# Attention and two gated FFNs on one core: the first four heads' gates by an added product, and the normalisation's small steps as one operation

## The chip, the cores and the metric

The kernel runs on one core of one Trainium2 chip, in one launch. The metric is the device time of the launch in microseconds (us); a kernel's time is the median of several runs. PE is TensorE, ACT is ScalarE, DVE is VectorE, POOL is GpSimd, and SP is the engine whose queue issues all DMAs here.

## What is computed

```python
# 4 batches, 8 heads, 576 tokens, head size 64
scores = q @ k.T / 8
cum    = np.cumsum(np.maximum(s, 0), axis=-1)              # gates, one row per head
scores = np.where(causal, -1e9, scores + np.minimum(-(cum[:, :, :, None] - cum[:, :, None, :]), 0))
attn   = np.exp(scores - scores.max(-1, keepdims=True))
attn   = attn / (attn.sum(-1, keepdims=True) + 1e-9)
x      = (attn @ v), heads side by side                    # 2304 tokens x 512
xn     = x / np.sqrt(np.mean(x * x, -1) + 1e-6) * rms_g
x      = (silu(xn @ w_gate) * (xn @ w_val)) @ w_out        # first FFN, 512 -> 1536 -> 512
out    = (silu(x @ w2_gate) * (x @ w2_val)) @ w2_out       # second FFN, no norm
```

All data are fp32. Because of the causal mask a query's own gate is a constant of its row, so only the keys' gates, less a common value, need to be added to the scores before the softmax.

## The kernel before

**Precision.** A dense product is made of three products of halves, high times high, low times high and high times low (`xH·H`, `xL·H`, `xH·L` in the rows). The weights are fetched raw and turned into the halves `H` and `L` on the chip by ACT (L384, L386, L396), DVE (L389, L392, L400) and POOL.

**Tiling.** Each batch's queries are two groups: A, the first 256 (tiles 0 and 1 of 128), and B, the other 320 (tiles 2 to 4). Group A of batches 0 and 1 is done first, as 16 early heads (`EarlyUnit`) in plain fp32 products. Then come the other groups head by head (`Head`, `Unit`).

**An early head.** `load` (L697) issues three DMAs: q and k transposed into rows 0 to 63 of a buffer `lq` (L701, 128 KB), the head's row of cumulated gates into row 64 of the key half (L705, 1 KB), and v into `vl` (L708). Row 64 of the query half holds ones and the rows behind are cleared by POOL (`clear_rows`, L457 and L458), so that the product over 128 rows adds each key's gate to its scores. `scores` (L711) makes two products, 128 x 128 and 128 x 256 (L716), into PSUM tiles `sps`. `least` (L601, DVE) adds the mask and finds each row's extreme in the same pass, and `exponent` (L612, ACT) writes the exponentials and their sums `tot`. `values` (L722) makes three transposes (L726), copies them to `pTA` (L731), makes the two products with v (L736) and copies the result into `x`. Two `lq` buffers of two halves each hold the loads of four heads.

**The gates.** The sequence `s` of all 32 heads is one 32 x 576 tile `cum`: clamped at zero (L473), cumulated by a scan (L476), reduced by its middle column and scaled (L481), all on DVE. It is stored to `cum_d` (L484) for the later heads.

**The normalisation** (`normalise`, L750) is called eight times, once for each group of each batch. ACT squares `x` (four operations), PE sums the squares with the constant `half` (L767) into one of four PSUM banks named `mo`, and 20 small steps of DVE (L795 to L829; tiles `fac`, `rc`, then the halves `sq`) make each token's factor for each head: inverse of the softmax sum, mean square, an inverse square root by three Newton steps, and the product of both. PE transposes the factors (L833), ACT copies them, PE spreads them over the rows by four products with the constant `sel` (L840), DVE multiplies `x` (L844), ACT and POOL or DVE make the halves `xH` and `xL` (L847, L849). Then the first FFN of this group may begin.

**The first FFN** (`moe1`): for each of 12 slices `f`, 12 products of `gate_value` (L860) fill one `mo` bank and 12 more a second one. `hidden` makes tanh (L867, ACT) and two operations of DVE (L869 `t`, L872 `hh`), which free the banks. `hh` is stored to `h_d`. The banks of the normalisation are out of the same four.

**What sets the order.** Nothing is issued as the code stands. Each operation is entered in a `Plan` with its engine, an assumed cost in ns, what it reads and writes, and a priority. `Plan.run` walks through an assumed time: an engine that is free takes the ready operation with the lowest priority value, and this writes out the fixed order of every engine. An operation entered as one is never split. `port=True` means that it isn't begun on DVE while POOL, by the plan, runs an operation. Each step of the normalisation is entered by itself:

```python
def step(fn, r=(), w=None):
    w = [col] if w is None else w
    op(DVE, TINY, fn, r=[*w, *r], w=w, pri=pri, port=True)   # TINY = 70
```

Of the kernel before, what the change touches and what calls it, by code (L numbers as in the profile page):

```python
# [251 lines left out]


@with_exitstack
def tile_kernel(
# [164 lines left out]

    mask = buf("at", "ft", [P, 2 * P], F32, "mask")

    def setup():
# [29 lines left out]

        def clear_rows(en):
            for b in early_q:
                for c in (0, 288):
                    en.memset(b()[D:, :, c:c + 256], 0.0)  # L457
                    en.memset(b()[D:D + 1, 0, c:c + 256], 1.0)  # L458
# [9 lines left out]
        def clear_scores(en):  # L468
# [4 lines left out]
        op(DVE, 400, lambda en: en.tensor_scalar(  # L473
            out=cum(), in0=cum(), scalar1=0.0, scalar2=None, op0=ALU.max),
           r=[cum], w=[cum], pri=-1e6)
        op(DVE, 670, lambda en: en.tensor_tensor_scan(  # L476
            cum2(), cum(), cum(), 0.0, op0=ALU.add, op1=ALU.max),
           r=[cum], w=[cum2], pri=-1e6)


        op(DVE, 400, lambda en: en.tensor_scalar(  # L481
            out=cum(), in0=cum2(), scalar1=cum2()[:, S // 2:S // 2 + 1], scalar2=1.0 / SCALE,
            op0=ALU.subtract, op1=ALU.mult), r=[cum2], w=[cum], pri=-1e6)
        op(SP, 4 * NB * NH * S, lambda en: en.dma_start(out=cum_d, in_=cum()),  # L484
           r=[cum], w=["cum_d"], pri=-1e6)
# [185 lines left out]
    class EarlyUnit(Unit):  # L671
# [6 lines left out]
        def __init__(self, b, h, x, tot):  # L678
# [8 lines left out]
            self.parts = lq_parts(early_q[i % 2], i // 2 % 2)  # L687
            self.vl = early_v[i % 2], i // 2 % 2
# [10 lines left out]
        def load(self, pri):  # L699
# [11 lines left out]
        def scores(self, pri):  # L711
            for t in self.tiles:
# [5 lines left out]
                    start=True, stop=True), r=[*self.parts, "lower rows"], w=[pt], pri=pri)  # L718
# [30 lines left out]
    def normalise(i, g, tot, pri):  # L749
# [42 lines left out]
        def u():  # L792
            return fac()[:, 1, :nt]
        F, U = (fac, 0), (fac, 1)
        step(lambda en: en.tensor_scalar(out=over(), in0=tot()[:, :nt], scalar1=1.0e-9,  # L795
                                         scalar2=None, op0=ALU.add), [tot], [F])
        step(lambda en: en.reciprocal(over(), over()), [], [F])
        step(lambda en: en.tensor_tensor(out=u(), in0=squares(), in1=over(), op=ALU.mult),
             [ps, F], [U])
# [342 lines left out]
```

## Time and profile before

| | |
|---|---|
| median of 3 runs | 1151.41 us (1149.88 to 1152.21) |
| the profiled execution's own time | 1150.37 us |
| its span, first to last instruction | 1148.4 us |
| mean granted clock of PE | 0.996 |
| PE busy | 1119.2 us, 97% of the span |
| DVE, ACT, POOL busy | 607.3, 545.7 and 188.9 us |

The profile is that of one execution. Its own time is 1.04 us below the median of the runs, and its span is 1.97 us shorter than its own time. Busy times are sums over the span; the stretches differ much, so they are read stretch by stretch in the rows below. Ends of products are modelled, since PE overlaps one product with the next.

### The profile page before, as it was taken

How to read it: one execution, taken by the hardware profiler on the slowest of the kernel's cores; microseconds unless marked ns; L12 is line 12 of the kernel's file. 1: busy time of each engine (PE TensorE's matmuls, PEld its weight loads, DVE VectorE, ACT ScalarE, POOL GpSimd, SP SyncE). 2: the span in 40 equal slices, each digit the busy share in tenths (PEclk: the TensorE clock that was granted, in tenths of full speed). 3: DMA queues.
4: the chain of work that ended last, by engine and by line, in shares of the span. 5: the costliest groups of instructions: out<-in, count | busy, mean ns of one | idle time of the engine just before them, and what ended most of it. 6: DMA issues, size and time to landing. Idle time of an engine off the chain costs nothing.

```text
span 1148.4 us, 18814 instructions
## 1 busy us (share of the span) xinstructions
PE 1119.2 (97%) x6708; PEld 1001.1 (87%) x6708; DVE 607.3 (53%) x1672; ACT 545.7 (48%) x1203; POOL 188.9 (16%) x282
## 2 busy tenths in 40 slices
PE   5889999999999999999999999999999999999998
PEld 3589999899999999999888788888888888888898
DVE  5898899979735875542686424432222222222222
ACT  5886889889434854431697435432111211211121
POOL 3343455354211300000021000001000100100000
PEclk9899999999999999999999999999999999999999
DMA  4874455334321223338756634211000100100000
GB/s 147 249 239 123 143 142 156 116 104 116 87 72 49 74 89 112 116 119 267 231 163 197 208 122 123 74 37 49 25 1 1 65 1 1 46 1 1 1 37 20
DMA packets 70221, 112.54 MB, mean 98 GB/s; under 512 B 11696, under 2 KB 39344, under 8 KB 70128
## 3 DMA queue, kind: packets, MB, share of 16 engines
q1 hardware_dynamic: 70128, 111.35, 31.6%
q8 instruction: 53, 0.87, 0.3%
q14 instruction: 40, 0.33, 0.1%
HBM read 87.63 MB, written 23.67 MB: 97 GB/s over the span
## 4 chain that ended last, share of the span: by engine, by line
PE 89%; DMA 3%; DVE 3%; ACT 2%; issue 1%; SPq 1%; POOL 0%; DVEq 0%; ACTq 0%
PE mo L860 50%; PE sps L1019 8%; PE tp L1019 8%; PE mo L1019 6%; PE sps L575 4%; PE tp L639 4%; PE tp L655 4%; DMA cvs<-in_w_gv 1%; PE mo L767 1%; PE tp L736 1%; PE sps L716 1%; DVE sc L601 1%; DMA hh<-h_d 1%; DMA lq<-cum 1%; PE tp L726 0%
## 5 line engine op out<-in xcount | busy, mean ns | idle before, releaser
L860 PE MATMUL mo<-xH,H 128*128 128x320 f32 (+1 forms) x768 | 228.1, 298 | 0.1
L860 PE MATMUL mo<-xL,H 128*128 128x320 f32 (+1 forms) x768 | 227.1, 296 | 0.5 <-POOL xL L849 0.5
L860 PE MATMUL mo<-xH,L 128*128 128x320 f32 (+1 forms) x768 | 227.0, 296 | 0.0
L869 DVE SCALAR_TENSOR_TENSOR t<-t,mo 128x256 f32<-128x256 f32 (+2 forms) x156 | 81.3, 521 | 257.7 <-ACT t L867 257.3
L867 ACT ACTIVATE t<-mo 128x256 f32<-128x256 f32 (+2 forms) x156 | 72.2, 463 | 284.8 <-PE mo L860 284.4
L860 PE MATMUL mo<-x1H,L 128*128 128x512 f32 (+1 forms) x480 | 176.6, 368 | 0.0
L860 PE MATMUL mo<-x1H,H 128*128 128x512 f32 (+1 forms) x480 | 176.6, 368 | 0.0
L860 PE MATMUL mo<-x1L,H 128*128 128x512 f32 (+1 forms) x480 | 176.6, 368 | 0.0
L1008 ACT ACTIVATE hH<-hh 128x512 fp32r<-128x512 f32 (+1 forms) x120 | 69.8, 585 | 169.4 <-DVE hh L872 133.1
L860 PEld LDWEIGHTS mo<-xL,H 128*128 128x128 f32 x768 | 144.2, 188 | 1.5 <-POOL xL L849 0.7
L860 PEld LDWEIGHTS mo<-xH,H 128*128 128x128 f32 x768 | 144.1, 188 | 1.0 <-issue 0.3
L860 PEld LDWEIGHTS mo<-xH,L 128*128 128x128 f32 x768 | 144.2, 188 | 0.4
L872 DVE TENSOR_TENSOR hh<-t,mo 128x256 f32<-128x256 f32 (+2 forms) x156 | 81.3, 521 | 99.4 <-PE mo L860 98.1
L1010 DVE TENSOR_TENSOR hL<-hh,hH 128x512 fp32r<-128x512 f32 (+1 forms) x120 | 79.6, 664 | 90.7 <-ACT hH L1008 90.3
L860 PEld LDWEIGHTS mo<-x1L,H 128*128 128x128 f32 x480 | 90.5, 189 | 15.0
L860 PEld LDWEIGHTS mo<-x1H,L 128*128 128x128 f32 x480 | 90.5, 189 | 14.9
L860 PEld LDWEIGHTS mo<-x1H,H 128*128 128x128 f32 x480 | 90.5, 189 | 14.7
L612 ACT ACTIVATE sc<-sc,col 128x512 f32<-128x512 f32 (+4 forms) x160 | 95.6, 598 | 15.6 <-DVE col L601 15.1
L1051 POOL TENSOR_TENSOR x1L<-x1l,x1H 128x512 fp32r<-128x512 f32 (+1 forms) x20 | 25.0, 1260 | 391.5 <-ACT x1H L1049 222.0
L639 PE MATMUL tp<-ident,sc 128*128 128x128 f32 x432 | 69.0, 278 | 1.3 <-DVE x L664 1.1
L1019 PE MATMUL sps<-hL,oH 128*128 128x512 f32 (+1 forms) x192 | 69.6, 364 | 0.1
L1019 PE MATMUL tp<-hL,oH 128*128 128x512 f32 (+1 forms) x192 | 69.4, 363 | 0.0
(129 smaller groups left out, 2097.0 us busy)
## 6 DMA issues: line engine op xcount, KB each, us to landing
raw<-in_w_gv SPq DMA_DIRECT2D x40, 512.0 KB, 4.8
cvs<-in_w_o SPq DMA_DIRECT2D x24, 512.0 KB, 3.7
hh<-h_d SPq DMA_DIRECT2D x48, 256.0 KB, 2.9
cb<-cum_d SPq DMA_DIRECT2D x32, 288.0 KB, 3.4
lq<-in_qk SPq DMA_DIRECT2D x32, 288.0 KB, 3.0
h_d<-hh SPq DMA_DIRECT2D x72, 128.0 KB, 2.2
vl<-in_vp SPq DMA_DIRECT2D x32, 160.0 KB, 3.1
cvs<-in_w_gv SPq DMA_DIRECT2D x8, 512.0 KB, 4.0
```

The source lines that it names most:

```text
L575: op(PE, c_mm(n), lambda en, pt=pt, o=o, c=c, n=n, z=z, kk=kk: en.matmul(pt()[:, :n], qst[j]()[:, o:o + 128], kk()[:, c:c + n], start=z == ...
L612: op(ACT, c_act(o + m, 2) + 35, lambda en: en.activation(sc()[:m, :o + m], sc()[:m, :o + m], ACTF.Exp, scale=-1.0, bias=col()[:m, 0, t:t + 1],
L639: op(PE, C_TR, lambda en, pt=pt, a=a, m=m, kb=kb, t=t: en.transpose(pt()[:, a:a + P], self.sc[t]()[:, kb * P:kb * P + P], ident()), r=[sel ...
L655: op(PE, c_mm(n), lambda en, w=w, z=z, kb=kb, d0=d0, n=n, o=o, kn=kn: en.matmul(po()[:, o:o + n], vst[j]()[:kn, kb, :], pT[g][z]()[:kn, d0 ...
L860: op(PE, c_mm(n), lambda en, a=a, x=x, c=c, k=k, i=i: en.matmul(ps()[:, :n], a()[:, c], x()[:, k, :n], start=(k == 0 and i == 0), stop=(k ...
L867: op(ACT, c_act(n), lambda en: en.activation(t()[:, :n], gp()[:, :n], ACTF.Tanh, scale=0.5), r=[gp], w=[t], pri=pri)
L869: op(DVE, c_tt(n), lambda en: en.scalar_tensor_tensor(out=t()[:, :n], in0=t()[:, :n], scalar=1.0, in1=gp()[:, :n], op0=ALU.add, op1=ALU.mu ...
L872: op(DVE, c_tt(n), lambda en: en.tensor_tensor(out=hh()[:, :n], in0=t()[:, :n], in1=vp_()[:, :n], op=ALU.mult), r=[vp_, t], w=[hh], pri=pri)
L1008: op(ACT, c_act(n) + 35, lambda en: en.activation(H()[:, :n], hh()[:, :n], ACTF.Copy), r=[hh], w=[H], pri=pri)
L1010: op(DVE, c_tt(n), lambda en: en.tensor_tensor(out=L()[:, :n], in0=hh()[:, :n], in1=f32(H()[:, :n]), op=ALU.subtract), r=[hh, H], w=[L], p ...
L1019: op(PE, c_mm(n), lambda en, d=d, c=c, w=w, x=x, i=i: en.matmul(acc_[d]()[:, :n], Wo[w]()[:, c], HL[x]()[:, :n], start=(f == 0 and i == 0) ...
L1051: op(POOL, c_ptt(n), lambda en, k=k, x=x: en.tensor_tensor(out=L()[:, k, :n], in0=x()[:, :n], in1=f32(H()[:, k, :n]), op=ALU.subtract), r= ...
```

## The change

1. The first four heads (`FIRST = 4`) get no row of gates by DMA. The cumulated gates of all 32 heads, for the first 256 keys, lie in a tile `cumA` of 128 rows, whose rows 32 to 127 are cleared by two memsets of POOL ahead of all other clearing. Behind each score product of these heads a second product adds `cumA`'s row of the head to all queries, with a column of the identity, spread, as the other operand. The other early heads' DMA reads its row out of `cumA`.
2. The three steps on the gates are made by `cumulate`, first for 256 columns into `cumA`, then once more for all 576 into `cum`, whose store to `cum_d` has a later priority.
3. In `normalise` two steps (the inverse) are one operation of the plan, and the other 18 are one, `factors`, entered at 170 ns for each step and without `port`.
4. The first FFN's weights have other priorities, both for the load and for the work on them.

```diff
+        def clear_cum(en):
+            en.memset(cumA()[NB * NH:64], 0.0)
+            en.memset(cumA()[64:], 0.0)
+        op(POOL, 500, clear_cum, w=[(cumA, 1)], pri=-2e6)
...
+        def cumulate(out, n, pri):
+            rows = NB * NH
+
+            def steps(en):
+                en.tensor_scalar(out=cum()[:, :n], in0=cum()[:, :n], scalar1=0.0, scalar2=None,
+                                 op0=ALU.max)
+                en.tensor_tensor_scan(cum2()[:, :n], cum()[:, :n], cum()[:, :n], 0.0,
+                                      op0=ALU.add, op1=ALU.max)
+                en.tensor_scalar(out=out()[:rows, :n], in0=cum2()[:, :n],
+                                 scalar1=cum2()[:, n // 2:n // 2 + 1],
+                                 scalar2=1.0 / SCALE, op0=ALU.subtract, op1=ALU.mult)
+            op(DVE, 400 + 3.6 * n, steps, r=[cum], w=[cum, cum2, (out, 0)] if out is not cum
+               else [cum, cum2], pri=pri)
+        cumulate(cumA, 2 * P, -1e6)
+        cumulate(cum, S, -900)
         op(SP, 4 * NB * NH * S, lambda en: en.dma_start(out=cum_d, in_=cum()),
-           r=[cum], w=["cum_d"], pri=-1e6)
+           r=[cum], w=["cum_d"], pri=-990)
...
-            op(SP, 1024, lambda en: en.dma_start(
-                out=ql()[D:D + 1, 1, 288 * i:288 * i + 256], in_=cum()[n:n + 1, 0:256]),
-               r=[cum, "lower rows"], w=self.parts[2:], pri=pri)
+            if not self.first:
+                op(SP, 1024, lambda en: en.dma_start(
+                    out=ql()[D:D + 1, 1, 288 * i:288 * i + 256], in_=cumA()[n:n + 1]),
+                   r=[cumA, "lower rows"], w=self.parts[2:], pri=pri)
...
+                if self.first:
+                    i = self.b * NH + self.h
+                    op(PE, 0.422 * 4 * kl, lambda en, pt=pt, kl=kl: en.matmul(
+                        pt()[:, :kl], ident()[:, i:i + 1].to_broadcast([P, P]), cumA()[:, :kl],
+                        start=False, stop=True), r=[ident, cumA], w=[pt], pri=pri)
...
-        def step(fn, r=(), w=None):
-            w = [col] if w is None else w
-            op(DVE, TINY, fn, r=[*w, *r], w=w, pri=pri, port=True)
+        chain = []
+
+        def step(fn):
+            chain.append(fn)
...
+        def inverse(en):
+            en.tensor_scalar(out=over(), in0=tot()[:, :nt], scalar1=1.0e-9, scalar2=None,
+                             op0=ALU.add)
+            en.reciprocal(over(), over())
+        op(DVE, 4 * TINY, inverse, r=[tot], w=[F], pri=pri, port=True)
...
+        def factors(en):
+            for fn in chain:
+                fn(en)
+        op(DVE, 170 * len(chain), factors, r=[ps, F], w=[col, fac, rr], pri=pri)
...
-        W1.append(load_gv(w_gv, f, places, tmps1, P_ATT + 10 + 0.5 * f,
-                          P_ATT - 1000 + 6 + 1.5 * f))
+        W1.append(load_gv(w_gv, f, places, tmps1, P_ATT + 12 + 0.5 * f,
+                          P_ATT - 1000 + 8 + 1.0 * f))
```

The costs and priorities change the order that the plan writes. On PE, at the very start of the program, the order before begins as follows (a number behind a name is that of the buffer's use; `lq_101` and `lq_106` are the first two heads):

```order
L716 MATMUL sps_165<-lq_101 128x128
L716 MATMUL sps_168<-lq_101 128x256
L716 MATMUL sps_177<-lq_106 128x128
L726 MATMUL tp_181<-ident,sc_170 128x128
L716 MATMUL sps_185<-lq_106 128x256
L726 MATMUL tp_181<-ident,sc_179 128x128 x2
```

After the change the same place on PE reads as follows, where L739 is the added product:

```order
L733 MATMUL sps_149<-lq_116 128x128
L733 MATMUL sps_162<-lq_116 128x256
L739 MATMUL sps_149<-cumA,ident 128x128
L739 MATMUL sps_162<-cumA,ident 128x256
L733 MATMUL sps_176<-lq_121 128x128
L739 MATMUL sps_176<-cumA,ident 128x128
L733 MATMUL sps_182<-lq_121 128x256
L749 MATMUL tp_187<-ident,sc_169 128x128
L739 MATMUL sps_182<-cumA,ident 128x256
```

Each score tile of the first four heads takes two products instead of one, eight added in all. On DVE, at the last of the eight normalisations, the 18 steps before stand among other work (L389 and L392 belong to weights, L872 to the first FFN). Nine of them stand here; nine more follow among other work, to L829:

```order
L798 TENSOR_TENSOR fac_5991<-mo_5931,fac_5991 128x24
L800 TENSOR_TENSOR fac_5991<-fac_5991 128x24
L872 TENSOR_TENSOR hh_6199<-t_6170,mo_6166 128x256
L801 TENSOR_REDUCE rc_6205<-fac_5991 128x3
L803 TENSOR_SCALAR rc_6205<-rc_6205 128x3
L805 TENSOR_SCALAR rc_6205<-rc_6205 128x3
L807 TENSOR_SCALAR rc_6205<-rc_6205 128x3
L810 SCALAR_TENSOR_TENSOR rc_6205<-rc_6205 128x3
L812 TENSOR_TENSOR rc_6205<-rc_6205 128x3
L389 TENSOR_SCALAR cvs<-cvs 128x512
L813 SCALAR_TENSOR_TENSOR rc_6205<-rc_6205 128x3
L392 SCALAR_TENSOR_TENSOR cvy<-cvy,cvs 128x512
```

After the change the 18 steps stand without a gap, and the FFN's two rows stand behind them; here is the end of the block:

```order
L836 SCALAR_TENSOR_TENSOR rc_6187<-rc_6187 128x3
L838 TENSOR_TENSOR rc_6187<-rc_6187 128x3
L839 SCALAR_TENSOR_TENSOR rc_6187<-rc_6187 128x3
L841 TENSOR_TENSOR fac_6001<-fac_6001,rc_6187 128x24
L854 CAST sq_87<-fac_6001 128x3x8
L855 TENSOR_TENSOR sq_87<-fac_6001,sq_87 128x3x8
L902 SCALAR_TENSOR_TENSOR t_6207<-t_6207,mo_6161 128x256
L905 TENSOR_TENSOR hh_6229<-t_6207,mo_6204 128x256
```

On PE, at the same normalisation after the change, 14 products of the FFN stand between the last sums of squares (L790) and the factors' transposes (L866); before the change 89 rows stand there. Of twelve rows with the same bank `mo_6204` the first three and the last three are shown:

```order
L790 MATMUL mo_5941<-half,sq_87 128x2 x3
L893 MATMUL mo_6161<-xL_517,H_1149 128x256
L893 MATMUL mo_6161<-xH_548,L_1195 128x256
L893 MATMUL mo_6204<-xH_548,H_1149 128x256
L893 MATMUL mo_6204<-xL_517,H_1149 128x256
L893 MATMUL mo_6204<-xH_548,L_1195 128x256
...
L866 MATMUL mo_6226<-ident,sq_87 128x128 x3
L893 MATMUL mo_6233<-xH_548,H_1283 128x256
```

So the transposes stand closer behind the sums than before. From the second FFN on, the order of every engine is the same.

## Rows read from the trace of the kernel before

**Rows 1.** The page, busy time of each engine over the span.

```profile
PE 1119.2 (97%) x6708; PEld 1001.1 (87%) x6708; DVE 607.3 (53%) x1672; ACT 545.7 (48%) x1203; POOL 188.9 (16%) x282
```

**Rows 2.** Windows: stretch, length, busy PE, PEld, DVE, ACT, POOL, PEclk, DMA, GB/s.

```profile
0.00:12.00 12.00, 0.23 (x1) 0.26 (x2) 4.66 (x15) 0.64 (x1) 6.41 (x21) 1.00 0.47 134
12.00:20.00 8.00, 7.30 (x24) 4.99 (x25) 4.05 (x17) 7.30 (x19) 1.27 (x1) 1.00 0.60 197
20.00:36.00 16.00, 15.34 (x90) 10.70 (x90) 13.14 (x48) 13.71 (x43) 4.41 (x5) 1.00 0.58 173
36.00:56.00 20.00, 15.78 (x73) 10.04 (x72) 16.61 (x60) 16.79 (x43) 7.09 (x9) 0.83 0.85 253
56.00:72.00 16.00, 13.31 (x99) 11.88 (x98) 14.59 (x33) 14.64 (x34) 6.39 (x9) 1.00 0.72 223
72.00:108.00 36.00, 35.14 (x286) 34.20 (x285) 32.08 (x95) 26.59 (x55) 15.64 (x15) 1.00 0.54 167
300.00:480.00 180.00, 179.47 (x1326) 176.84 (x1326) 111.52 (x349) 86.45 (x208) 26.21 (x45) 1.00 0.27 80
```

**Rows 3.** Timeline of the start: start, us, engine, line, operation, what ended idle time.

```profile
1.64 0.65 SPq L701 DMA_DIRECT2D lq<-in_qk  x1
3.19 0.86 DVE L473 TENSOR_SCALAR cum<-cum 32x576 f32<-32x576 f32 x1
4.09 1.35 DVE L476 TENSOR_TENSOR_SCAN cum<-cum 32x576 f32<-32x576 f32 x1
3.80 0.51 POOL L458 MEMSET lq<- 1x256 f32 x1
4.37 0.32 POOL L462 MEMSET mask<- 128x256 f32 x1
5.74 0.39 POOL masks.py:199 TENSOR_SCALAR_AFFINE_SELECT ident<-ident 128x128 f32<-128x128 f32 x1
7.62 2.49 SPq L705 DMA_DIRECT2D lq<-cum  x4
11.36 1.28 ACT L384 ACT_TABLE_LOAD   x1 [11.36 <-DMA raw<-in_w_gv]
11.77 2.08 PE L716 MATMUL sps<-lq 128*128 128x128 f32 x6 [11.77 <-DMA lq<-cum]
13.94 0.37 ACT L612 ACTIVATE sc<-sc,col 128x128 f32<-128x128 f32 x1
```

**Rows 4.** DMA view to 80 us: issues, KB each, us to landing.

```profile
lq<-in_qk SPq DMA_DIRECT2D x16, 128.0 KB, 2.9
```

**Rows 5.** Timeline of PE: one early head's two score products, twice.

```profile
16.07 1.53 PE L716 MATMUL sps<-lq 128*128 128x128 f32 x4
21.82 0.82 PE L716 MATMUL sps<-lq 128*128 128x128 f32 x4
```

**Rows 6.** Timeline of the first normalisation on PE and DVE.

```profile
37.45 0.61 PE L767 MATMUL mo<-half,sq 128*128 128x2 f32 x4
38.31 0.18 DVE L800 TENSOR_TENSOR fac<-fac 128x16 f32<-128x16 f32 x1
50.84 0.17 DVE L829 TENSOR_TENSOR sq<-fac,sq 128x16 f32<-128x16 f32 x1
51.28 0.69 PE L833 MATMUL mo<-ident,sq 128*128 128x128 f32 x2
56.51 0.36 PE L860 MATMUL mo<-xH,H 128*128 128x256 f32 x1
```

**Rows 7.** Timeline of DVE: small steps of a later normalisation.

```profile
302.52 0.18 DVE L801 TENSOR_REDUCE rc<-fac 128x3 f32<-128x24 f32 x1
302.63 0.49 DVE L872 TENSOR_TENSOR hh<-t,mo 128x320 f32<-128x320 f32 x1
303.04 0.16 DVE L803 TENSOR_SCALAR rc<-rc 128x3 f32<-128x3 f32 x1
303.24 0.17 DVE L805 TENSOR_SCALAR rc<-rc 128x3 int32<-128x3 int32 x1
```

**Rows 8.** Timeline around the fourth normalisation's transposes, and a wait before it.

```profile
216.15 0.76 PE L639 MATMUL tp<-ident,sc 128*128 128x128 f32 x5 [1.11 <-DVE x L664]
...
224.44 1.40 POOL L529 TENSOR_TENSOR qst<-lq,qst 64x576 fp32r<-64x576 f32 x1 [2.30 <-DMA cb<-cum_d]
224.45 1.43 DVE L829 TENSOR_TENSOR sq<-fac,sq 128x24 f32<-128x24 f32 x1
225.94 0.55 PE L833 MATMUL mo<-ident,sq 128*128 128x128 f32 x3 [0.78 <-DVE sq L829]
```

**Rows 9.** The chain of waits: start, us, what; 131 products in a row.

```profile
80.75 15.43 PE mo L860 x131
```

**Rows 10.** Timeline of DVE near the last normalisation.

```profile
420.84 0.42 DVE L869 SCALAR_TENSOR_TENSOR t<-t,mo 128x256 f32<-128x256 f32 x1 [1.49 <-ACT t L867]
```

More of the change, by code (lines that the diff above doesn't have):

```diff
@@ L251 @@
 TINY = 70
+FIRST = 4
 @with_exitstack
@@ L419, in tile_kernel @@
     cum = buf("at", "pTB0", [NB * NH, S], F32, "cum")
+    cumA = buf("at", "pTB1", [P, 2 * P], F32, "cumA")
     mask = buf("at", "ft", [P, 2 * P], F32, "mask")
@@ L472, in setup @@
         op([(POOL, 1500), (DVE, 1500)], 0, clear_scores, w=sc4, pri=-1e5)
[L473 to L483, printed above, removed]
+        def cumulate(out, n, pri):
[12 more added lines that the diff above has]
+        cumulate(cum, S, -900)
         op(SP, 4 * NB * NH * S, lambda en: en.dma_start(out=cum_d, in_=cum()),
-           r=[cum], w=["cum_d"], pri=-1e6)
+           r=[cum], w=["cum_d"], pri=-990)
     def lq_parts(b, half):
@@ L687, in __init__ @@
             self.parts = lq_parts(early_q[i % 2], i // 2 % 2)
+            self.first = i < FIRST
             self.vl = early_v[i % 2], i // 2 % 2
@@ L717, in scores @@
                     pt()[:, :kl], self.qk(0)[:, o:o + P], self.qk(1)[:, :kl],
-                    start=True, stop=True), r=[*self.parts, "lower rows"], w=[pt], pri=pri)
+                    start=True, stop=not self.first), r=[*self.parts, "lower rows"], w=[pt],
+                   pri=pri)
+                if self.first:
[3 more added lines that the diff above has]
+                        start=False, stop=True), r=[ident, cumA], w=[pt], pri=pri)
                 self.least(pt, t, 0, 0, kl, mask, True, True, pri, P - o)
@@ L793, in u @@
             return fac()[:, 1, :nt]
[L794 to L799, printed above, removed]
-        step(lambda en: en.tensor_tensor(out=u(), in0=u(), in1=over(), op=ALU.mult), [F], [U])
+        F = (fac, 0)
+        def inverse(en):
[3 more added lines that the diff above has]
+        op(DVE, 4 * TINY, inverse, r=[tot], w=[F], pri=pri, port=True)
+        step(lambda en: en.tensor_tensor(out=u(), in0=squares(), in1=over(), op=ALU.mult))
+        step(lambda en: en.tensor_tensor(out=u(), in0=u(), in1=over(), op=ALU.mult))
         step(lambda en: en.tensor_reduce(out=m(), in_=u(), axis=mybir.AxisListType.X,
-                                         op=ALU.add), [U])
+                                         op=ALU.add))
         step(lambda en: en.tensor_scalar(out=m(), in0=m(), scalar1=1.0 / DM,
@@ L817, in normalise @@
             in1=y().rearrange("p (t o) -> p t o", o=1).to_broadcast([P, nt, NH]),
-            op=ALU.mult), [col], [F])
+            op=ALU.mult))
         rr = sq[1]
@@ L827, in columns @@
             return rr().rearrange("p (t h) -> p t h", h=P)[:, :nt, NH * z:NH * z + NH]
-        step(lambda en: en.tensor_copy(columns(0).bitcast(F32R), over()), [F], [rr])
+        step(lambda en: en.tensor_copy(columns(0).bitcast(F32R), over()))
         step(lambda en: en.tensor_tensor(out=columns(1), in0=over(), in1=columns(0),
-                                         op=ALU.subtract), [F], [rr])
+                                         op=ALU.subtract))
+        def factors(en):
+            for fn in chain:
+                fn(en)
+        op(DVE, 170 * len(chain), factors, r=[ps, F], w=[col, fac, rr], pri=pri)
         tp = mo_bank()
```

## The prediction

> **What bounds the kernel now.** The page's busy times come first: PE works in 97% of the span, no other engine in more than 53% [rows 1]. So in most of the program a change is worth only what it does to PE: products added, or waits and slow stretches taken away. The windows by stage tell where PE has either [rows 2]. In the first 12 us it works 0.23 us. From 36 to 56 us it idles 20 − 15.78 = 4.22 us at a granted clock of 0.83, and from 56 to 72 us 2.69 us. In the 180 us from 300 to 480, where the last two normalisations lie, it idles 0.53 us in all. Gains can therefore come from the first 72 us alone; behind them a new wait of PE is a loss in full. From the second FFN on the order is the same, so whatever the front gives or costs is carried to the end.
>
> The timeline of the start shows why PE waits [rows 3]: the gates are scanned until 5.44 us, then SP issues four 1 KB rows from 7.62 to 10.11, and the first product starts at 11.77, released by that row. The q and k of the first head were asked for at 1.64.
>
> **A. The start (−5.0, at best −6.4).** For the first four heads that row is gone. The first product then needs q and k and cleared rows: issue from 1.64 for 0.65, then 2.9 us to landing [rows 3, 4], so 4.5 to 5.2; the clearing ends at 3.80 + 0.51 = 4.31, and the two new memsets ahead of it cost some 0.3 each by the mask's memset of 0.32 [rows 3], so about 4.9. The added product also needs the identity, ready at 6.13, or 6.8 behind the memsets. The gates themselves are no later: 256 columns of three steps that take 2.72 us for 576 are some 1.3 us, done near 4.5, and the second pass over 576 columns ends near 7.2. First product near 5.1, which is 6.7 earlier; first complete tile near 7.1, `least` at 7.3. Then ACT: its table load of 1.28 us ran from 11.36, behind a wait for the weights, and the first exponential came at 13.94 [rows 3]. The order now puts that load ahead of the first exponential; if it shares that one's wait, the exponential comes at 7.6 + 1.3 = 8.9, or 5.0 earlier, else at 7.6, 6.3 to 6.4 earlier. I take −5.0, since the load waited with the instruction behind it before too.
>
> **B. The eight added products (+3.3, at most +6.1).** They have the shapes of the heads' own two, which take 1.53 us a head near 16 us and 0.82 near 22 [rows 5]. Four heads are 6.1 or 3.3. From 12 to 20 us PE is at work in 7.30 of 8 us [rows 2], so they aren't hidden. The slow figure holds for some eight microseconds behind the first product; these four heads lie in such a stretch in part, but their own scores and the later heads move out of it likewise, so the cost in the end is the fast one.
>
> **C. The first normalisation (−2.5, between 0 and −3.2).** Its steps spread from the sums at 37.45 to the last one's end at 51.01 because each lets other DVE work pass, and the first FFN product comes at 56.51 [rows 6]. In a later normalisation a dependent step starts 0.20 us behind the one before (303.04 to 303.24) and another operation 0.11 behind (302.52 to 302.63) [rows 7]. 18 steps in a block are 3.6 us, with 0.45 for the way in and out about 4. The FFN could start near 44 less the gain of A, and its products would fill the 6.9 us of idle PE and lift the clock. But in these 36 us ACT works 16.79 + 14.64 = 31.4 and DVE 31.2 [rows 2]: ACT has 4.6 free, DVE 4.8, and the FFN's first slices give both more work. A gathered step costs 0.09 more than one with a stranger behind it, 1.6 us for 18, which leaves 3.2 of DVE. So 3.2 bounds the gain; I take 2.5, nearer to it than to nothing, as some PE idle is certain to be filled.
> The Trainium skill speaks against even that price (VectorE: DVE Perf Modes, The DRAIN you can't avoid): each operation's pipe empties before the next begins, and chaining without semaphores saves nothing. By it a gathered step costs no more than a spread one, the bound is ACT's 4.6, and the sum would be about 1.4 us lower; the 0.11 against 0.20 of the trace speaks for the dearer reading.
> The weights' changed priorities move conversions of ACT and DVE by a slice or so inside the same stretch. I price them at nothing, because the same work lies before 108 us, where DVE has 3.9 us free [rows 2]; without that cover one conversion late costs up to a microsecond.
>
> **D. The seven later normalisations (+4.0, between +2.2 and +8).** The block is not split, so PE needs work for 3.6 + 0.45 = 4.05 us between the last sums and the factors' transposes (L866). Counting products in the changed order and pricing them at 15.43/131 = 0.118 us for 256 columns [rows 9] and the like for others, PE has about 6.9, 3.6, 4.8, 4.05 and 4.0 us at the second to sixth, 24 products or 2.9 us at the seventh, and 14 or 1.7 us at the eighth. The waits are 0, 0.45, 0, 0, 0.05, 1.15 and 2.35: 4.0. More products aren't to be had there: two of the four banks wait for `t` and `hh`, which now stand behind the block on DVE and take 0.42 [rows 10] and about as much again. For that I add 1.0, some 0.25 at four of them. Off come the stalls that the spread steps make now: 0.78 at 225.94, where the last step collided with POOL, and some of the 1.11 at 216.15 [rows 8], in all 1.0. So +4.0. The lower end is the last two waits without the banks, 3.5 − 1.3. The upper end counts the banks double and adds collisions: the last step took 1.43 us beside POOL's L529 instead of 0.18 [rows 7, 8], and the block no longer keeps clear of POOL; two or three times 1.25 is 2.5 to 3.75, so about 8.
> Here the Trainium skill agrees with the trace (SBUF — State Buffer, Terms): DVE and POOL share a port pair, and the loser blocks for the other's whole instruction.
>
> **The sum.** −5.0 + 3.3 − 2.5 + 4.0 = −0.2 us on the profiled execution's own 1150.37, so 1150.2; the median of the runs stands 1.04 above that execution, so 1151.2. A difference under 0.2%, 2.3 us, can hardly be told from none here.
>
> **The rivals.**
> *The front gives more (faster, 0.33).* The table load doesn't wait (−6.4), the idle stretch fills to its bound (−3.2), the later waits keep to the low end: −6.4 + 3.3 − 3.2 + 2.2 = −4.1, so 1147.3. For it: 11.8 us of idle PE at the start and 6.9 from 36 to 72 are more than I count. Against: ACT and DVE are nearly full there.
> *The block stalls the later stages (slower, 0.22).* With the collisions D is 8, and the sum −4.2 + 8 = +3.8, so 1155.2. It decides from D above 6.5, three collisions. For it: PE idles 0.53 us in 180 now, so nothing absorbs a wait; the one collision in the trace hit the very last step. Against: POOL is busy 26 of 180 us where the two barest normalisations lie [rows 2].
> *The change doesn't do what it says at the front (slower, 0.05).* The heads start earlier, but the added products run at the slow 6.1, and the later heads' rows, still by DMA, and weights keep the first FFN product where it was: −5.0 + 6.1 + 0 + 4.0 = +5.1, so 1156.5.
> *The two cancel, as forecast (within 0.2%, 0.40).*
>
> **The range.** The forecast's own reach is 1149 to 1153.5. To hold 8 in 10 it goes to the first two rivals' sums and a bit over: 1146 to 1156. Faster by over 0.2% 0.33, same 0.40, slower 0.27.
>
> **What would show it.** A: the first product near 5 us, the first `least` near 7.3, the first exponential at 7.6 or 8.9. B: eight rows of L739, 0.8 or 1.5 us a head. C: the first block some 3.6 us long, the first FFN product before 46 us, less idle and a higher clock in 36 to 72. D: waits of PE at L866, released by DVE, near 1.2 us at the seventh normalisation and 2.4 at the eighth, and a step of over 1 us beside POOL only if the second rival holds. **I would be wrong** if PE didn't wait at the last two, which would make the kernel faster by some 4 us, or if the first FFN product didn't move, which would make it slower.

## The result and the profile after

The changed kernel is slower: 1161.71 us (median of 4 runs, 1160.2 to 1164.0) against 1151.34 for the kernel before, a ratio of 1.0094 with a 95% interval of 1.0080 to 1.0108. The profiled execution took 1160.2 us, its span 1158.4. The forecast was 1151.2, its range ended at 1156.

The timeline of the start, which answers to [rows 3]:

```profile
0.72 1.28 ACT L627 ACT_TABLE_LOAD   x1 [0.72 <-PEq L1165]
4.74 1.62 PE L733 MATMUL sps<-lq 128*128 128x128 f32 x4 [4.74 <-POOL lq L467]
6.97 1.65 PE L739 MATMUL sps<-cumA,ident 128*128 128x128 f32 x4 [0.60 <-POOL ident masks.py:199]
7.80 0.29 DVE L616 CUSTOM_DVE_ANT_0 sc<-sps,mask 128x128 f32<-128x128 f32 x1 [0.44 <-PE sps L739]
8.14 0.40 ACT L627 ACTIVATE sc<-sc,col 128x128 f32<-128x128 f32 x1 [6.13 <-DVE col L616]
```

The start does what was forecast: the first product comes 7.0 us earlier, the first exponential 5.8 us earlier. The windows (columns as in [rows 2]) show where the time is lost again:

```profile
36.00:56.00 20.00, 18.78 (x130) 15.90 (x130) 17.82 (x56) 19.39 (x50) 8.86 (x9) 1.00 0.84 263
72.00:108.00 36.00, 30.71 (x236) 29.83 (x237) 28.23 (x74) 19.15 (x39) 14.71 (x17) 0.95 0.42 127
300.00:480.00 180.00, 173.25 (x1246) 168.82 (x1245) 117.04 (x379) 92.81 (x226) 32.53 (x53) 0.98 0.29 86
```

From 36 to 56 us PE idles 1.22 us at full clock, where before it idled 4.22 at 0.83. But from 72 to 108 us it idles 5.29 (before 0.86), from 300 to 480 us 6.75 (before 0.53). The view of PE's waits to 480 us names the cause in its first line (who waited for whom, us in total, times, longest):

```profile
PE mo L866 <- DVE sq L855: 15.9, 7, 5.1
```

L866 is the factors' transposes, L855 the last of the 18 gathered steps. The second normalisation shows how the longest of these waits comes about; the timeline of PE, VectorE and GpSimd:

```profile
62.33 0.95 PE L790 MATMUL mo<-half,sq 128*128 128x2 f32 x8
64.93 1.46 DVE L394 SCALAR_TENSOR_TENSOR cvy<-cvy,raw 128x512 int32<-128x512 int32 x1
67.14 2.92 POOL L402 TENSOR_TENSOR L<-cvy,H 128x512 fp32r<-128x512 f32 x2 [1.29 <-ACT H L398]
67.89 0.17 DVE L825 TENSOR_TENSOR fac<-mo,fac 128x16 f32<-128x16 f32 x1
68.09 0.74 DVE L826 TENSOR_TENSOR fac<-fac 128x16 f32<-128x16 f32 x1
69.07 1.01 DVE L829 TENSOR_SCALAR rc<-rc 128x2 f32<-128x2 f32 x1
70.13 0.88 POOL L544 TENSOR_TENSOR qst<-lq,qst 64x320 fp32r<-64x320 f32 x1
70.32 0.72 DVE L833 TENSOR_SCALAR rc<-rc 128x2 int32<-128x2 int32 x1
71.09 1.42 POOL L547 TENSOR_TENSOR kLL<-lq,kHH 128x576 fp32r<-128x576 f32 x1
71.27 1.25 DVE L838 TENSOR_TENSOR rc<-rc 128x2 f32<-128x2 f32 x1
74.97 0.17 DVE L855 TENSOR_TENSOR sq<-fac,sq 128x16 f32<-128x16 f32 x1
75.29 0.56 PE L866 MATMUL mo<-ident,sq 128*128 128x128 f32 x2 [5.08 <-DVE sq L855]
```

The block runs from 67.89 to 75.14, 7.25 us. Steps that otherwise take 0.16 to 0.18 us last as long as GpSimd's subtraction beside them still runs: one is held up, mostly a single one passes at its end, and the next is held up by GpSimd's next subtraction. Free of these subtractions, at the first, fifth, seventh and eighth normalisation, the blocks take 3.65, 3.58, 3.67 and 3.73 us, as the 18 × 0.20 of [rows 7] said; the second, third, fourth and sixth take 7.25, 5.14, 5.98 and 6.46. Together that is 10.4 us more than four of 3.6. The waits at L866 are 0.94, 5.08, 1.59, 2.41, 0.11, 2.76, 0.92 and 2.15 us, from the first normalisation to the eighth.

The longest wait has a second cause. The sums of squares (L790) end at 63.28, but VectorE, at work on the weights (L394), begins the block 4.61 us later; at six of the other seven normalisations it begins within 0.05 us, at the fifth after 0.47. Meanwhile PE uses up the products that stand between the sums and the transposes, 75.29 − 63.28 − 5.08 = 6.93 us of them. An estimate from these rows: without the collisions, with a block of 3.6 us, this wait would have been 1.4 us; without the late start 0.5.

Then there is a part that the prediction didn't have. The windows behind the wait that ended at 75.29, microsecond by microsecond:

```profile
75.00:76.00 1.00, 0.71 (x4) 0.60 (x5) 0.91 (x4) 0.11 (x1) 0.00 (x0) 0.71 0.00 0
76.00:77.00 1.00, 1.00 (x6) 1.00 (x6) 0.32 (x1) 1.00 (x3) 0.00 (x0) 0.50 0.50 152
77.00:78.00 1.00, 1.00 (x5) 0.90 (x4) 0.61 (x2) 0.66 (x2) 0.00 (x0) 0.50 0.86 209
78.00:79.00 1.00, 1.00 (x7) 1.00 (x7) 0.27 (x1) 1.00 (x3) 0.60 (x1) 0.59 0.93 266
79.00:80.00 1.00, 1.00 (x10) 0.96 (x9) 0.83 (x3) 0.72 (x2) 0.83 (x2) 1.00 0.83 295
```

PE is busy again from 75.3 on, but at a granted clock of 0.50, 1.2 GHz in place of 2.4, until about 78.9; it works on 5 to 7 products in a microsecond instead of 10. In this execution the same happens behind the waits of 2.41, 2.76 and 2.15 us, and not behind those of 1.59 us and less.

### The profile page after: what moved, and what is told of

Read it like the earlier page. It is cut to its first block, busy times and chain, and to the rows that moved or that the text cites. A ratio compares the mean times of both kernels' runs of the same rounds, so it can differ in the third digit from the quotient of the medians.

```text
span 1158.4 us, 18902 instructions
## 1 busy us (share of the span) xinstructions
PE 1125.2 (97%) x6724; PEld 1007.6 (87%) x6724; DVE 619.0 (53%) x1663; ACT 547.4 (47%) x1204; POOL 199.9 (17%) x295
## 4 chain that ended last, share of the span: by engine, by line
PE 59%; DMA 2%; DVE 2%; ACT 1%; issue 0%; DVEq 0%; ACTq 0%
PE mo L893 36%; PE sps L1052 9%; PE tp L1052 9%; PE mo L1052 5%; DMA cvs<-in_w_gv 1%; DVE cvy L394 0%; ACT cvy L386 0%; DVE hL L1043 0%; DMA cvs<-in_w_o 0%; ACT hH L1041 0%; DMA hh<-h_d 0%; DVE L L402 0%; DVE raw L391 0%; ACT cvy L388 0%; PE mo L790 0%
## 5 line engine op out<-in xcount | busy, mean ns | idle before, releaser
L893 PE MATMUL mo<-xL,H 128*128 128x320 f32 (+1 forms) x768 | 229.5, 299 | 0.4 <-DVE xL L882 0.4
```

What stands on the lines that cost most here:

```text
L893: op(PE, c_mm(n), lambda en, a=a, x=x, c=c, k=k, i=i: en.matmul(ps()[:, :n], a()[:, c], x()[:, k, :n], start=(k == 0 and i == 0), stop=(k ...
```

## The experiments

Each ratio is to the kernel before, in runs on the same chip, with its 95% interval; 0.001 is 1.15 us. A difference of two ratios carries both intervals, which makes its own 95% interval some ±2 to ±3 us. A trace is that of one execution. "The front alone" is the first kernel below.

**The front alone, and the block alone.** The first takes the gathering of the steps out of the change, as the diff shows; the second puts nothing but the gathering into the kernel before:

```diff
-        chain = []
-
-        def step(fn):
-            chain.append(fn)
+        def step(fn, r=(), w=None):
+            w = [col] if w is None else w
+            op(DVE, TINY, fn, r=[*w, *r], w=w, pri=pri, port=True)
...
-        op(DVE, 170 * len(chain), factors, r=[ps, F], w=[col, fac, rr], pri=pri)
```

> The changed kernel with the normalisation's 20 small steps entered one by one again, as before; the added products, the two cumulations and the weights' priorities stay. Theory (the block of 18 steps makes the loss, in 15.9 us of PE's waits at the factors' transposes and the slow clock behind them, and the front gains): 1141 to 1146, 6 to 10 below the kernel before, and the waits of PE on the factors under 2 us in all. Rival (the front itself costs, by its products and the other order of the weights, and the block is about neutral): 1157 to 1162.

Measured: 0.9979 (0.9969 to 0.9990). The front gains, 2.4 us, but not the 6 to 10 expected. PE is busy for 1125.4 us here and for 1125.2 in the changed kernel, in spans of 1144.4 and 1158.4: the 14 us between the two traces are idle time of PE.

> The kernel before with the gathered steps alone. Theory: the loss stands without the front's gain, 15 us or more above before, 1164 to 1172, with PE waiting over 12 us for the factors. Rival (the block is about neutral, the front costs): 1149 to 1154.

Measured: 1.0194 (1.0169 to 1.0219), 22 us slower; PE waits 15.0 us for the factors, at all eight normalisations. The loss is the block's. In this order less PE work lies between sums and transposes than in the changed kernel at some places, at the second normalisation 1.9 us instead of 6.9; that alone doesn't account for 22 against the 13 that the block costs with the front, and the rest of that difference wasn't pursued.

**GpSimd out of the way.** Three kernels. The first asks the plan to keep the block clear of GpSimd:

```diff
-        op(DVE, 170 * len(chain), factors, r=[ps, F], w=[col, fac, rr], pri=pri)
+        op(DVE, 170 * len(chain), factors, r=[ps, F], w=[col, fac, rr], pri=pri, port=True)
```

> The changed kernel, with the block of 18 steps not begun by the plan while GpSimd works, as the single steps were. Theory that the collisions with GpSimd are the larger part: if the plan's order keeps them apart on the chip, the four long blocks fall from 5.1 to 7.3 us toward 3.6, PE's waits on the factors from 15.9 toward 6, and the time to 1149 to 1153. Rival (the block's length and place make the waits, not GpSimd): within 2 us of the changed kernel, 1160 to 1163. If the engines' real times run away from the plan's, the collisions stay, and the time too; the trace tells the two apart.

Measured: 1.0100 (1.0082 to 1.0119), as the changed kernel. The blocks at the second, third, fourth and sixth normalisation still take 6.8, 5.5, 6.0 and 4.8 us: the plan's order holds nothing apart on the chip, where nothing but the data makes an engine wait for another. The run says nothing on the collisions' price.

The second leaves the order alone and changes what GpSimd does in its subtractions:

```diff
+    def keep(en, out, in_, dims):
+        en.affine_select(out=out, in_=in_, pattern=[[0, d] for d in dims], base=1,
+                         compare_op=ALU.is_ge, fill=0.0, channel_multiplier=0)
...
-            op([(POOL, c_ptt(n)), (DVE, c_tt(n))], 0, lambda en: en.tensor_tensor(
+            op([(POOL, c_ptt(n)), (DVE, c_tt(n))], 0, {DVE: lambda en: en.tensor_tensor(
                 out=kl()[:, :n], in0=ql()[:, 1, :n], in1=f32(kh()[:, :n]), op=ALU.subtract),
+                POOL: lambda en: keep(en, kl()[:, :n], ql()[:, 1, :n], [n])},
```

> The changed kernel in the same order, but GpSimd's subtractions of two inputs are replaced by a selection with one input that passes it on; the low halves that GpSimd makes are left out so. Theory (collisions): all eight blocks take 3.6 to 3.8 us, PE's waits on the factors fall from 15.9 to 5 to 7, the time to 1148 to 1152. Rival (the block's length and its late start alone): blocks shorter, but the time above 1157.

> The control for the run in which GpSimd passes one input on: the same replacement in the kernel with the front alone, whose steps are single (the low halves that GpSimd makes are left out). If the 12 us that the replacement took off the changed kernel were the price of collisions within the blocks, this one moves by under 3 us, to 0.995 to 0.999 of before. If shorter work of GpSimd gains by itself wherever it stands, it falls by 8 or more, to 0.990 or below.

Measured: 0.9989 (0.9977 to 1.0001) with the block, 0.9962 (0.9946 to 0.9977) with the front alone. The replacement takes 12.1 us off the kernel with the block and 2.0 off the one without. The difference, 10 us (±3), is what GpSimd's subtractions cost by way of the blocks beyond what the selections cost there, the slow clock behind the waits included. All blocks now take 3.6 to 4.4 us, and PE's waits on the factors shrink:

```profile
PE mo L872 <- DVE sq L861: 5.7, 5, 2.2
```

The one input isn't what does it. The timeline of the second normalisation shows steps that last to the end of the selection beside them (L277 is the helper `keep`):

```profile
70.95 0.69 POOL L277 TENSOR_SCALAR_AFFINE_SELECT kLL<-lq 128x576 fp32r<-128x576 f32 x1
71.14 0.52 DVE L839 TENSOR_SCALAR rc<-rc 128x2 int32<-128x2 int32 x1
71.60 0.48 POOL L277 TENSOR_SCALAR_AFFINE_SELECT vst<-vl 128x320 fp32r<-128x320 f32 x1
71.69 0.39 DVE L842 SCALAR_TENSOR_TENSOR rc<-rc 128x2 f32<-128x2 f32 x1
```

A selection holds a step up as a subtraction does, but it is half as long (0.69 us instead of 1.44 for `kLL`, on average). The pair of runs prices GpSimd's time beside the blocks, not its second input.

The third keeps GpSimd's work whole and moves the steps' operands instead, with the same operations in the same order:

```diff
+        def small():
+            return ps()[:, 64:73].rearrange("p (a b) -> p a b", b=3)
+
         def m():
-            return col()[:, 0, :nt]
+            return small()[:, 0, :nt]
...
         def u():
-            return fac()[:, 1, :nt]
+            return ps()[:, 128:128 + nt * NH].rearrange("p (t h) -> p t h", h=NH)
```

> The changed kernel in the same order on every engine, with most of the steps' operands in the PSUM bank of the squares' sums, so that a step reads at most one operand from SBUF; the result is computed in full. Theory (a step is held up by GpSimd where it reads two operands, or one of plain form, from SBUF): the blocks by GpSimd's work shorten to within 1 us of the others, PE's waits on the factors fall to some 7, and the time to about 0.999 to 1.003 of before, less whatever a PSUM operand costs (18 steps by some 0.05 is 0.9 a block). Rival (GpSimd holds VectorE up whatever the operands are): 1.009 as the changed kernel.

Measured: 1.0034 (1.0021 to 1.0047), 6.9 us less than the changed kernel. The blocks by GpSimd's work take 5.65, 3.76, 4.58 and 5.14 us, so two of the four stay more than 1 us above the others, and PE waits 9.4 us for the factors, not some 7. The timeline at the second normalisation (two rows) and at the fourth:

```profile
69.22 2.93 POOL L402 TENSOR_TENSOR L<-cvy,H 128x512 fp32r<-128x512 f32 x2 [1.30 <-ACT H L398]
71.01 1.16 DVE L836 TENSOR_SCALAR rc<-rc 128x2 int32<-128x2 int32 x1
...
222.85 1.43 POOL L547 TENSOR_TENSOR kLL<-lq,kHH 128x576 fp32r<-128x576 f32 x1 [2.59 <-DMA cb<-cum_d]
222.95 0.16 DVE L842 SCALAR_TENSOR_TENSOR rc<-mo,rc 128x3 f32<-128x3 f32 x1
223.14 0.17 DVE L839 SCALAR_TENSOR_TENSOR mo<-rc,mo 128x3 f32<-128x3 f32 x1
223.34 0.17 DVE L841 TENSOR_TENSOR mo<-mo,rc 128x3 f32<-128x3 f32 x1
224.36 1.43 POOL L544 TENSOR_TENSOR qst<-lq,qst 64x576 fp32r<-64x576 f32 x1
224.78 1.06 DVE L858 TENSOR_TENSOR sq<-fac,sq 128x24 f32<-128x24 f32 x1
```

Beside L547 the steps with one operand in PSUM (`mo`) and one in SBUF run at 0.16 to 0.17 us. The last step, both of whose operands lie in SBUF, is held up by L544 for 1.06. At the second normalisation L836 is held up as well, for 1.16, with one operand, in SBUF. No step of this run's blocks that reads an operand from PSUM took over 0.19 us. So an operand in PSUM keeps a step clear of GpSimd, and two operands in SBUF aren't needed for it to be held up.

**The clock behind the waits.** Spare products of constants keep PE at work ahead of four of the waits:

```diff
+    FILL = {2: 36, 4: 16, 6: 18, 8: 13}
...
+            def turn(en, c=c):
+                for _ in range(more if c == 0 else 0):
+                    en.matmul(tp()[:, :256], sel()[:, 0:2].rearrange("p h d -> p (h d)"),
+                              sel()[:, 0:4].rearrange("p h d -> p (h d)"), start=True, stop=True)
+                en.transpose(tp()[:, c * P:c * P + P], rr()[:, c * P:c * P + P], ident())
```

> The changed kernel in the same order, with spare products of constants put right ahead of the factors' transposes of the second, fourth, sixth and eighth normalisation (36, 16, 18 and 13, at 0.118 us each 4.2, 1.9, 2.1 and 1.5 us), where PE waited 5.1, 2.4, 2.8 and 2.2 us; the result doesn't change. PE has no less to wait for, but doesn't idle. Theory (behind each of these waits the clock falls to half for some 3.5 us, and that costs another 1.7 us each): 1154 to 1157, 5 to 7 below the changed kernel, 1.003 to 1.005 of before, without half-clock stretches behind them. Rival (the slow stretches cost nothing, or come whatever PE does in the wait): 1160 to 1163.

Measured: 1.0059 (1.0037 to 1.0081), 4.0 us (±3) faster than the changed kernel, in which PE has less to do. The clock stays at 1.00 behind all four places; PE's remaining waits for the factors are 5.8 us. The slow clock costs some 4 us of the changed kernel's time, less than the 5 to 7 expected.

How long PE waits doesn't settle whether the clock falls. The 4 us behind the eighth normalisation's wait of 2.15 us, in the changed kernel and, with the same wait at the same place, in the kernel with four blocks below:

```profile
430.20:434.20 4.00, 4.00 (x21) 4.00 (x22) 2.52 (x6) 0.70 (x2) 0.00 (x0) 0.57 0.34 88
425.44:429.44 4.00, 4.00 (x30) 3.68 (x31) 3.78 (x8) 0.91 (x2) 0.00 (x0) 1.00 0.38 98
```

In the kernels with the block alone and with `port` too the clock stayed full behind a wait of 2.15 us at this place, and it fell behind one of 1.83 us at the second normalisation of the kernel with selections.

**Bare blocks, with the front.** Steps are gathered at some normalisations only (`BLOCKS` holds 1, 5, 7 and 8, or 8; for the first alone it is 1, compared with `<=`):

```diff
+        block = normalised[0] in BLOCKS
```

> The changed kernel with the steps gathered at the first normalisation alone; the other seven have single steps as before. It tests the predicted gain of the first block (2.5 us). If that holds, it lies 1.5 to 3 us below the kernel with the front alone, at about 0.9955 of before, with the first FFN product some 5 us earlier. Rival (ScalarE and VectorE are full in this stretch, so the earlier FFN gives nothing): within 1 us of the front alone, 0.997 to 0.999.

Measured: 0.9975 (0.9965 to 0.9985). Within the uncertainty this is the front alone. The first FFN product comes at 41.12 instead of 49.70, and the clock from 36 to 56 us is 1.00 instead of 0.74; but from 72 to 108 us PE idles 5.28 us instead of 1.80, at a clock of 0.91 instead of 1.00, and the waits name a new releaser, ScalarE's conversion of the weights:

```profile
PE mo L906 <- ACT H L400: 4.1, 4, 1.7
```

> The kernel with the front alone, and the steps gathered at the first, fifth, seventh and eighth normalisation, where no GpSimd work met the block in the changed kernel; single steps at the other four. If GpSimd's collisions are most of the loss, and the block's bare length costs what the trace shows there (waits of 0.9, 0, 0.9 and 2.2): 3 to 5 us over the front alone (0.9979 of before), 1.000 to 1.003. If gathering itself loses, wherever it is done: half of the 13 us, 1.004 or above.

Measured: 1.0056 (1.0041 to 1.0071), 8.9 us over the front alone: a miss, and what was expected if gathering loses wherever it is done (1.004 or above). No block met a subtraction of GpSimd (3.65, 3.73, 3.66 and 3.73 us long). PE waits 0.93, 1.85, 0.91 and 2.15 us ahead of the four transposes, 5.8 in all; at the fifth normalisation 18 products (2.6 us) lie between sums and transposes here, 28 (4.1 us) in the changed kernel. The waits for ScalarE's conversions stand in this trace as with the first block alone (4.1 us).

> The kernel with the front alone and the steps gathered at the eighth normalisation only; the order is that of the front alone until there. It prices the bare block at the place with the least work to cover it. Theory: wait 2.2 and the half clock behind it 1.7, so 3.5 to 5.5 over the front alone (0.9979 of before): 1.001 to 1.0027. The prediction's price for this place was 2.35 and part of 1.0: 1.000.

Measured: 1.0042 (1.0025 to 1.0059), 7.2 us (±2.3) for one block at the eighth normalisation, not to be told apart from the 8.9. The block takes 3.73 us; PE waits 3.5 us for it here, 2.2 in the changed kernel, since 2 products lie between sums and transposes here and 14 there. So it isn't the changed kernel's eighth block that this run prices. The windows of four microseconds around it show that wait and then the half clock:

```profile
416.00:420.00 4.00, 4.00 (x37) 4.00 (x36) 0.78 (x4) 2.43 (x5) 0.00 (x0) 1.00 0.39 125
420.00:424.00 4.00, 0.60 (x5) 0.39 (x4) 3.06 (x19) 1.18 (x3) 0.00 (x0) 0.61 0.00 0
424.00:428.00 4.00, 3.92 (x20) 3.92 (x21) 2.60 (x7) 0.42 (x2) 0.00 (x0) 0.53 0.35 101
428.00:432.00 4.00, 4.00 (x32) 3.79 (x31) 1.46 (x3) 0.79 (x3) 0.00 (x0) 1.00 0.73 232
```

Some 2.7 us more of waits stand 170 to 270 us later: from 500 to 760 us PE waits 3.6 us for the halves of the hidden rows (`hH`, `hL`), 0.9 with the front alone. They lie in the products of the first FFN's output, all but one before 655 us, where the order of PE, ScalarE and VectorE isn't that of the front alone; on PE it is the same only from 667 us on. The kernel with the first block alone has 2.9 us of such waits too and is as fast as the front alone, so that the last block costs 2.7 us there isn't shown.

> The same with 13 spare products (1.5 us) in the wait ahead of the factors' transposes. If the clock's part is real, 1.3 to 2 us faster than the one without; if not, the same or slower.

Measured: 1.0039 (1.0024 to 1.0054). The profiled executions differ by 3.7 us in span and the clock stays full behind the wait in the filled one, but that one is the fastest of its kernel's runs, 2.8 us below their median, and over the runs the two can't be told apart. Whether the half clock costs time at this place stays open.

**The parts of the front.** All with single steps, and with the weights' old priorities:

```diff
-        W1.append(load_gv(w_gv, f, places, tmps1, P_ATT + 12 + 0.5 * f,
-                          P_ATT - 1000 + 8 + 1.0 * f))
+        W1.append(load_gv(w_gv, f, places, tmps1, P_ATT + 10 + 0.5 * f,
+                          P_ATT - 1000 + 6 + 1.5 * f))
```

> The kernel with the front alone, but the weights' priorities of before. The prediction priced them at nothing: then 0.997 to 0.999 of before. If the new priorities cost, it is faster than the front alone by over 1.2 us, 0.9965 or below; if they gain, 0.999 or above.

Measured: 0.9964 (0.9952 to 0.9977), against 0.9979 with the new priorities. The intervals overlap: the new ones cost 1.7 us (±1.9), which may be nothing.

> The kernel with the front alone and the weights' old priorities, but no head gets the added product: the gates are cumulated for 256 columns first, and all 16 early heads get their row by DMA. It tells what the first four heads' product gains on balance. Theory (start earlier by 5 to 6 us, eight products cost some 2 to 3): the time goes back to 0.999 to 1.001 of before, with the first product near 10 us. Rival (the gain of the front is from the shorter first cumulation and the later store of the gates): stays at 0.995 to 0.998.

Measured (`FIRST = 0`): 0.9989 (0.9977 to 1.0000). The first product comes at 8.79 and the first exponential at 10.06. So the shorter steps ahead of the rows, together with the table load that no longer waits (0.73), bring 3.9 us of the 5.8 by which the exponential moved, but the product is worth 2.9 us (±2) at the end.

> The kernel with the front alone and the old weights' priorities, with each of the eight added products made twice (the second one adds rows of zeros; the result is the same). It doubles the disputed cost. If the products lie on the path at their full price, the time rises by 3 to 6 us over the kernel with them once (0.9964 of before), to 0.999 to 1.002. If PE would have waited for ScalarE and VectorE there, it rises by under 1.5 us, 0.9965 to 0.998.

Measured: 0.9960 (0.9946 to 0.9974). Doubling the added products costs nothing that these runs can tell (−0.5 us, ±2).

> The kernel with the front alone and the old weights' priorities, with the added product for eight heads instead of four. As products made twice cost nothing, more heads without the gates' row could start earlier: if the 1 KB rows still hold later heads up, 0.9945 to 0.996 of before; if the heads behind the fourth are held by ScalarE and VectorE, the same as with four, 0.9955 to 0.9975.

Measured (`FIRST = 8`): 0.9966 (0.9953 to 0.9980), the same as with four.

**A version meant to be fast.**

> A version meant to be fast: the front alone, old weights' priorities, single steps, their operands in the squares' PSUM bank as far as possible. The one step that GpSimd held up before goes shorter, but the bank is held until the last Newton step, which takes one of four banks from the first FFN for 5 to 15 us in each normalisation. If the bank matters, slower than with SBUF operands: 0.998 or above; if not, 0.995 to 0.997.

Measured: 1.0009 (0.9995 to 1.0022), 5 us slower than its parent. The small steps gain nothing in PSUM when they stand apart, and holding the bank longer fits the loss, though no row was followed for it. The fastest that the experiments point to is the front with the old priorities and single steps, 0.9964, with the added product made once.

## Why the prediction was wrong

**Term D failed.** It was +4.0, at most +8; the block costs 13.2 us beside the front (1.0094 against 0.9979). Its mechanism, waits of PE at the transposes in the later normalisations, is what the trace shows, and the price without collisions was near at the seventh and eighth: 1.15 and 2.35 forecast, 0.92 and 2.15 found. But at the second to fourth and the sixth it forecast 0.50 in all, and 11.84 came. Four things were missing from it.

- *Collisions with GpSimd, as a rule and not an accident.* I counted them in the upper bound alone, two or three of 1.25 us. Half of the blocks met GpSimd's subtractions, for 3.6, 1.5, 2.4 and 2.9 us; with the shorter selections in their place the block costs 10 us less. The one collision of before [rows 8] should have been weighed by what surrounds it: twelve of the 18 steps have two operands in SBUF, and steps with a single one were held up too (L829, 1.01 us, and L833, 0.72); while GpSimd goes from one subtraction to the next, the block advances by a step or two for each of them. GpSimd's busy time from 300 to 480 us, 26 us of 180, was right for the seventh and eighth normalisation, which met none of its work, but the wrong measure for the others: it works where heads are prepared, which is where the second, third, fourth and sixth normalisation stand. The Trainium skill (VectorE: DVE Perf Modes, Two Vector instructions with no wait between them) says which operand is concerned: the second SBUF read interface is shared with GpSimd; an instruction with two SBUF tensors reads the second through it, and one in a two-port mode its first. The run with operands in PSUM agrees (0.16 us beside a subtraction of 1.43, and 1.06 for the step with two SBUF operands). For the steps with one operand (L829, L833; 1.16 us at L836 of that run) no trace shows the mode.
- *The block's start.* D let the block begin at the sums, with 0.45 us for the way in and out. At six of the seven later normalisations that was about right (0.04 us in, 0.47 at the fifth, and up to 0.15 out); at the second the block began 4.61 us late, behind VectorE's work on the weights, and the 6.9 us of products, counted rightly, were used up before it was done. At the fourth the count itself was off: 4.8 us of products forecast, 3.8 found.
- *The clock behind a wait.* In D a wait cost its own length. Behind four of the eight, of 2.15 us and more, PE ran at half clock for 3.4 us each, and keeping it at work there gave back 4.0 us (±3). In three other traces a wait of 2.15 us at the same place had no such stretch behind it. Set against the front alone this part is smaller: its trace has a half-clock stretch of 10.2 us at the first normalisation, which the block removed. The Trainium skill (TensorE: Matmul & The Clock Gate, Part 1: The HAM clock gate) states that the array's clock is gated between half and full by how busy PE has been of late; the rows agree in kind.
- *The rest of the first FFN.* One block at the eighth normalisation costs 7.2 us (±2.3), in an order with fewer products to cover it: in its trace the wait of 3.5, a half-clock stretch of 6.8, and 2.7 us more of waits for the halves of the hidden rows. D looked at the normalisations alone and took the order as the same from the second FFN on, as it is; but most of the first FFN's output products come before it, and there the order had changed. What that costs by itself stays open.

The second rival was the right one in kind, and its sign, steps of over 1 us beside GpSimd, is there; its point of decision, D above 6.5, was passed twofold, and its 0.22 was too little. Neither of the two signs that I had named for being wrong appeared. (D's lower end takes off 1.3 us of stalls where the text has 1.0; nothing hangs on it.)

**Term A was right at the start and came to half at the end.** Forecast for the first exponential: 7.6 or 8.9; found: 8.14, since the table load runs at 0.72 without waiting; the step in which it would share the exponential's wait was wrong. Of the 5.8 us the front alone keeps 2.4 to 4.1.

**Term B was too dear.** The eight products were priced at 3.3 us; made twice they cost nothing more that the runs can tell, which fits time in which PE would have waited anyway; no run shows where. A and B together, −1.7 by the forecast, were measured at −2.4 with the new priorities: the sum was right by luck, its terms weren't.

**Term C brought no gain that the runs can tell.** The block at the first normalisation is 3.65 us long and brings the FFN's first product 8.6 us earlier (in the changed kernel it comes at 40.06; the forecast was 44 less the gain of A), but the end moves by 0.5 us (±1.7; 0.9975 against 0.9979). The bound was read from ScalarE's and VectorE's free time; in the trace the gain goes again where the FFN, started earlier, reaches slices whose weights ScalarE hasn't converted yet (4.1 us of waits, and a half-clock stretch of 6.8 us behind them). The first rival, which counted on this term, fell with it.

**The weights' priorities**, priced at nothing, cost 1.7 us (±1.9).

The parts don't add up to the last microsecond: collisions 10 and one bare block 7 are more than 13. The bare blocks were measured in other orders (7.2 us for one, 8.9 for four), in which less work covers some of them. In the changed kernel's own order the run with selections on GpSimd lies 3.1 us (±2.2) above its control: that is near what the blocks cost there beyond the collisions. How it divides among the eight places wasn't measured, and which of the other orders' costs are waits, half clock or later waits is read from one trace each.

## What to carry to other kernels

Before many short VectorE operations are joined to one that nothing can interrupt, look at what GpSimd does in that stretch: a step whose operands lie in SBUF can wait until GpSimd's operation beside it ends, and a chain of them turns into a chain of such waits; one operand in PSUM took the steps here out of it, and shorter work on GpSimd shortened the waits. Count the work that the bounding engine has between the input of the chain and its use, and from the moment at which the chain really begins. Price a wait of TensorE of some two microseconds or more at its length, with half clock behind it as a risk: in these traces it came behind some such waits and not behind others. A plan's rule that keeps two engines apart holds only on the plan's own time axis, unless data make one wait for the other.

## What the hardware showed that was not expected

- A single VectorE step of 0.17 us can be held up to 1.43 us by a GpSimd subtraction, and with back-to-back subtractions the engines take turns: mostly one or two steps, one subtraction. With one of two operands in PSUM a step isn't held up, and costs no more (0.16 to 0.19 us).
- A selection with one input on GpSimd holds such steps up too, until it ends: 0.52 us beside a selection of 0.69. It costs less because it is shorter: with selections in place of the subtractions the sixth block took 4.0 us instead of 6.46.
- In the changed kernel the granted clock was 0.50 for 3.4 us behind waits of PE of 2.15 to 5.08 us, and 1.00 behind waits of 0.92, 0.94 and 1.59 us. In other traces it stayed at 1.00 behind waits of 2.15 us (three times at the eighth normalisation) and fell behind one of 1.83: the wait's length alone doesn't tell.
